# Issue order and PSUM bank of each job from two written tables instead of a list scheduler

## The chip, the cores and the metric

The kernel runs on one core of one Trainium2 chip. The metric is the device time of one execution in microseconds (us); the median of three runs is given.

## The reference

Linear attention of the Linformer kind for 8 batches, 8 heads, 1024 positions and a head width of 64, then a gated feed-forward layer. All inputs and the output are float32.

```python
k_proj = einsum('ks,bhsd->bhkd', E, k)          # 64 projected keys per head
v_proj = einsum('ks,bhsd->bhkd', F, v)
scores = (1/8) * q @ k_proj^T                   # 1024 x 64 per head
attn   = exp(scores - max); attn = attn / (sum(attn) + 1e-9)
x      = attn @ v_proj                          # heads side by side: 8192 x 512
gate   = 1 / (1 + exp(-(x @ w_gate)))           # 512 x 1536
val    = x @ w_val
out    = (gate * val) @ w_out                   # 1536 x 512
```

## The kernel before

Tokens are worked in 16 blocks of 512, two to a batch. Each batch has an attention part: `kv` projects keys and values on TensorE, ScalarE copies the result out (`kd`, `vd`), a transposing DMA or TensorE turns it (`turnk`), `sc` makes the scores of 128 tokens and four heads, VectorE takes the maximum (`top`) and it is subtracted (`sub`, on TensorE or VectorE), ScalarE takes the exponential (`exp`), a DMA turns it (`turnp`), `xo` multiplies by the values, VectorE inverts the sums (`inv`), VectorE or GpSimd divides (`div`), and a DMA turns the result (`turnx`) into the input of the feed-forward part.

The feed-forward matrix products of a block use a Strassen-like scheme with seven products in place of eight (`seven`, L1162). In `quad_jobs` a step has one such scheme for the gate (jobs `G...`) and one for the value (jobs `V...`); the names A11, A12, A22, S1 to S4 tell which product it is. Each product is four matmuls of 256 columns. Between products ScalarE copies a half-made PSUM bank away (`snap`, `copy`), VectorE adds such copies (`plus`), ScalarE takes `tanh`, and VectorE multiplies gate and value (`hidden`). The output product is in `o_jobs` (seven products, jobs `O...` of six matmuls each) or, for the first and last block, in `o_plain` (`Oplain`, twelve matmuls). Results leave PSUM by `leave` and `merge` and go out by `store`.

Work is cut into 2,902 jobs, numbered from 0 in the order in which the code makes them; "sc16" below is job 16, of the kind `sc`. A job has an engine, a position and a body that issues its instructions: 1,054 jobs for TensorE, 712 for ScalarE, 814 for VectorE, 167 for GpSimd (POOL) and 155 for SyncE. Every engine carries out its own jobs strictly in the order in which they are issued. `Plan` (L55) derives every semaphore wait from what each instruction reads and writes, DMAs included, so it needs no change when the order changes.

A job's PSUM result lies in one of 8 banks and its float32 scratch in one of 13 buffers; until the order is known they are `Slot`s, gathered into groups. `Scheduler.run` (L331) sets the order: a list scheduler that keeps a clock for every engine by estimated costs, places the ready job with the lowest position on a free engine, and picks a free bank or buffer (`take`, L264) with a check that no group can lock the others out (`safe`). The positions come from the tables `AT` and `FB` of numbers. Before 25 us of its clock, when TensorE has no ready job, it places a filler: two 128-column matmuls of the identity into bank 7 that nothing reads (`busy(2)`). 45 fillers are placed.

The first batch has a path of its own (`first_batch`, L786): `pk` and `pv` project keys and values as their loads land, `tq` and `tk` turn queries and keys on TensorE, `psum` and `norm` sum and divide on VectorE or GpSimd, `tp` turns the result, `xo0` multiplies by the values; `pkk`, `tqk`, `tkk`, `pvk`, `tpk`, `xok` are the copies out of PSUM. The first block's gate and value products are plain (`plainG`, `plainV`; here G and V with the job's number). `wsum`, `osum`, `xs` and `sum` make the sums that the seven-product scheme needs. Loads of the next batch (`loadkv`, `loadq`) are jobs of GpSimd's queue and wait until the batch before has been turned (`turnx`).

Of the kernel before, what the change touches and what calls it, by code (L numbers as in the profile page):

```python
# [153 lines left out]
class Job:  # L154
    def __init__(self, eng, pos, body, release, name):
        self.eng, self.pos, self.body, self.release, self.name = eng, round(pos, 6), body, release, name
        self.cost, self.bytes, self.dma, self.port = 0.0, 0, False, False
        self.deps, self.slots, self.start, self.end = {}, [], None, None


class Scheduler:

    TAIL = {"PE": 0.0, "ACT": 0.115, "DVE": 0.09, "POOL": 0.15, "SP": 0.0}
    HOP = {"PE": 0.205, "ACT": 0.035, "DVE": 0.035, "POOL": 0.06, "SP": 0.1}

    EXTRA = dict(
        qt=0.12, qt1=0.16, turnk=0.1, turnk0=0.1, tp=0.1, tx=0.1, tk=0.1, tq=0.1, bc0=0.8, den0=0.2, xo0=0.2,
        copyG=0.028, copyV=0.028, copyO=0.028, tanh=0.015, kd=0.1, vd=0.1,
    )

    def __init__(self, banks, bufs, t0, window, landed, busy0, warm):
        self.jobs, self.now, self.t0, self.window, self.landed = [], None, t0, window, landed
        self.busy0, self.warm, self.fillers = busy0, warm, []
        self.writers, self.readers = {}, {}
        self.free = {
            "bank": {b: t0 for b in banks},
            "buf": {b: t0 for b in bufs},
        }
        self.clean = {b: False for b in banks}
        self.groups = []  # L180
        self.reads = []
        self.more = {"ACT": AT["pact"], "DVE": AT["pdve"], "POOL": AT["ppool"]}

    def job(self, eng, pos, body, release=0.0, name=""):
        j = Job(eng, pos, body, release, name)
        self.jobs.append(j)
        self.now = j
        body()
        j.cost += self.EXTRA.get(name, 0.0)
        self.now = None  # L190
        return j

    def note(self, eng, r, w, x, dma, cost, nbytes, port):
        j = self.now
        j.port = j.port or port
        assert eng == j.eng, (eng, j.eng, j.name)
        j.cost += cost
        j.bytes += nbytes
        j.dma = j.dma or dma is not None

        def dep(o, raw):
            if o is not j:
                j.deps[o] = j.deps.get(o, False) or raw

        for k in tuple(r) + tuple(w) + tuple(x):
            if isinstance(k, tuple) and isinstance(k[1], Slot) and k[1] not in j.slots:
                j.slots.append(k[1])
                k[1].left += 1
        for k in r:
            if k in self.writers:  # L210
                dep(self.writers[k], True)
        for k in tuple(w) + tuple(x):
            if k in self.writers:
                dep(self.writers[k], False)
            for o in self.readers.get(k, ()):
                dep(o, False)
        for k in r:
            self.readers.setdefault(k, []).append(j)
        for k in tuple(w) + tuple(x):
            self.writers[k] = j  # L220
            self.readers[k] = []

    def seen(self, o, eng, raw):
        if o.dma:
            return o.end + 0.1
        if o.eng == eng:
            if eng == "PE":
                return o.start + o.cost
            return o.end + 0.02
        if o.eng in ("ACT", "DVE", "POOL") and eng == "PE":  # L230
            return o.end + 0.055
        return o.end + self.HOP[o.eng]

    def safe(self, group, got):
        left = {k: len(f) for k, f in self.free.items()}
        left["clean"] = sum(self.clean[b] for b in self.free["bank"])
        for g, b in got:
            left[g.kind] -= 1
            if g.kind == "bank":
                left["clean"] -= self.clean[b]  # L240
        taken = [g for g, _ in got]
        todo = []
        for g in self.groups + ([] if any(group is x for x in self.groups) else [group]):
            need, held = dict.fromkeys(left, 0), dict.fromkeys(left, 0)
            for x in g:
                if x.at is None and not any(x is y for y in taken):
                    need[x.kind] += 1
                    need["clean"] += x.clean
                elif x.left:
                    held[x.kind] += 1  # L250
                    held["clean"] += x.kind == "bank" and not x.dirty
            todo.append((need, held))
        while todo:
            for i, (need, held) in enumerate(todo):
                if all(need[k] <= left[k] for k in left):
                    for k in left:
                        left[k] += held[k]
                    del todo[i]
                    break
            else:  # L260
                return False
        return True

    def take(self, j, t):  # L264
        got = []
        for s in j.slots:
            if s.at is not None:
                continue
            taken = [b for g, b in got if g.kind == s.kind]
            mine = [b for b, a in self.free[s.kind].items() if a <= t and b not in taken]  # L270
            if s.kind == "bank":
                if s.clean:
                    mine = [b for b in mine if self.clean[b]]
                elif s.dirty:
                    rough = sum(not c for c in self.clean.values()) + sum(self.clean[b] for _, b in got)
                    mine = [b for b in mine if not self.clean[b] or rough < (7 if t < 25.0 else 3)]
                mine.sort(key=lambda b: (self.clean[b], self.free["bank"][b]))
            else:
                mine.sort(key=lambda b: self.free["buf"][b])
            if not mine:  # L280
                return False
            got.append((s, mine[0]))
        if not got:
            return True
        group = got[0][0].group
        if not self.safe(group, got):
            return False
        if not any(group is g for g in self.groups):
            self.groups.append(group)
        for s, b in got:  # L290
            s.at = b
            del self.free[s.kind][b]
            if s.dirty:
                self.clean[b] = False
        return True

    def running(self, j):
        return any(x.group is g for x in j.slots for g in self.groups)

    def place(self, j, t):  # L300
        j.start = t
        j.cost *= 1 + self.more.get(j.eng, 0.0)
        if j.port:
            if j.eng == "DVE":
                j.cost += max(0.0, self.held - t)
                self.lock = t + j.cost
            if j.eng == "POOL":
                j.cost += max(0.0, self.lock - t)
                self.held = t + j.cost
        j.end = t + j.cost + self.TAIL[j.eng]  # L310
        if j.dma:
            begin = max(self.pipe, t + j.cost + 1.3)
            self.pipe = begin + j.bytes / 390e3
            j.end = self.pipe + 0.9 + AT["pdma"]
        self.busy[j.eng] = t + j.cost
        for s in j.slots:
            s.left -= 1
            s.end = max(s.end, j.end + (0.25 if j.eng == "PE" else 0.055))
            if s.left == 0:
                self.free[s.kind][s.at] = s.end  # L320
                if s.kind == "bank" and not s.clean:
                    self.clean[s.at] = not s.dirty
                if all(x.at is not None and not x.left for x in s.group):
                    self.groups = [g for g in self.groups if g is not s.group]
        for k in self.after.get(j, ()):
            self.count[k] -= 1
            if self.count[k] == 0:
                ready = max([self.seen(o, k.eng, raw) for o, raw in k.deps.items()] + [k.release, self.t0])
                self.open[k.eng].append((k.pos, self.rank[k], ready, k))

    def run(self):  # L331
        engines = ("PE", "ACT", "DVE", "POOL", "SP")
        self.busy = dict(self.busy0)
# [4 lines left out]
        for j in self.jobs:  # L338
            self.count[j] = len(j.deps)
            for o in j.deps:  # L340
                self.after.setdefault(o, []).append(j)
# [44 lines left out]
def bass_linformer_attn__then__ffn_glu_sigmoid_kernel(  # L386
# [20 lines left out]
    with contextlib.ExitStack() as es:  # L407
# [62 lines left out]
        NB = 11  # L470
# [1444 lines left out]
```

## Time and profile before

| what | value |
|---|---|
| median of 3 runs | 518.52 us (518.36 to 518.65) |
| span of the profiled execution | 517.0 us |
| median less this span | 1.5 us |
| first matmul to last matmul's end, in the profile | 5.5 to 514.4 us |
| TensorE busy | 508.4 us, 98% |
| VectorE busy | 444.8 us, 86% |
| ScalarE busy | 375.4 us, 73% |
| GpSimd busy | 171.6 us, 33% |
| filler matmuls | 90 of 128 columns |

The profile's times are in microseconds from the start of the span. A row of a timeline gives the start, the time to the end of the last merged instruction, the engine, the source line, the operation, what is written and read, and how many instructions were merged; in brackets, the engine's idle time before it and what ended that. A row of the table of stretches gives the stretch and its length, then the busy time and number of instructions of TensorE, of its weight loads (PEld), of VectorE, ScalarE and GpSimd, then the granted TensorE clock (1.00 is full), the DMA's share in tenths as a mean, and GB/s. L528 is the line of the helper that issues every matmul, L542 of every ScalarE instruction. The profile shows the time to a matmul's modelled end, so consecutive matmuls overlap, and their spacing is read from the starts. The profiled execution has no time of its own beside the span; it is set against the median of the runs.

### The profile page before, as it was taken

Reading aid. Unit: us, or ns where it says so; the run is one execution under the profiler, and the core shown is the slowest. Engines: PE = TensorE matmul, PEld = TensorE weight load, DVE = VectorE, ACT = ScalarE, POOL = GpSimd, SP = SyncE. Lnnn points to the kernel's source line nnn. Section 1 sums busy time; section 2 is a strip of 40 time slices with the busy share of each in tenths; the row PEclk is TensorE's granted clock in tenths of the full one; section 3 lists DMA queues with packets and bytes.
Section 4 is the critical chain, followed back from the end, with each engine's and each line's share of the span. In section 5 each row is a group of like instructions: output and inputs, shape, how many; then the busy total and the mean of one; then the engine's idle time right before and its main releaser. Section 6 shows DMA issues by size and latency. Waiting matters only on the chain.

```text
span 517.0 us, 12313 instructions
## 1 busy us (share of the span) xinstructions
PE 508.4 (98%) x4786; PEld 428.2 (83%) x4786; DVE 444.8 (86%) x843; ACT 375.4 (73%) x715; POOL 171.6 (33%) x200
## 2 busy tenths in 40 slices
PE   5999999999999999999999999999999999999997
PEld 4655867889988898888988889888998889888885
DVE  5879998898999799996999969997999969999570
ACT  1566966879977697777967689776877779677752
POOL 9882004802353024430344313630244303403200
DMA  9999928796689636994489926997369963610204
GB/s 160 198 198 207 202 64 161 117 215 136 123 174 203 161 58 129 187 185 132 82 160 170 191 76 95 188 204 146 77 113 183 202 143 62 145 42 1 82 1 164
DMA packets 140522, 71.59 MB, mean 138 GB/s; under 512 B 97200, under 2 KB 132272, under 8 KB 140464
## 3 DMA queue, kind: packets, MB, share of 16 engines
q0 software_dynamic: 35904, 29.89, 37.4%
q1 hardware_dynamic: 104560, 40.91, 36.9%
q8 instruction: 38, 0.62, 0.5%
q14 instruction: 20, 0.16, 0.1%
HBM read 60.29 MB, written 16.78 MB: 149 GB/s over the span
## 4 chain that ended last, share of the span: by engine, by line
PE 93%; DVE 5%; DMA 1%; ACT 0%; issue 0%; POOL 0%; SPq 0%
PE pA L528 47%; PE pF L528 46%; DVE topf L1645 1%; DVE hT L1066 1%; DMA EF<-in_F_dram 1%; DVE pA L1672 1%; DVE pF L1672 1%; DVE inv L989 0%; ACT KVs L542 0%; POOL wT L996 0%; DVE tG L557 0%; ACT ost L542 0%; DVE inv L990 0%; DVE eT L886 0%; DVE xT L886 0%
## 5 line engine op out<-in xcount | busy, mean ns | idle before, releaser
L542 ACT ACTIVATE spare<-pF 128x512 f32<-128x512 f32 (+2 forms) x167 | 93.7, 572 | 30.5 <-PE pF L528 27.6
L557 POOL TENSOR_TENSOR hT<-hT,hS 128x512 bf16<-128x512 bf16 x42 | 48.6, 1184 | 193.7 <-PE pA L528 155.1
L542 ACT ACTIVATE spare<-pA 128x512 f32<-128x512 f32 (+2 forms) x150 | 85.1, 582 | 15.6 <-PE pA L528 12.0
L542 ACT ACTIVATE spare<-spare 128x512 f32<-128x512 f32 x77 | 48.5, 635 | 25.7 <-DVE spare L1156 25.4
L1734 POOL TENSOR_TENSOR KVs<-spare,inv 128x384 bf16<-128x384 f32 (+1 forms) x50 | 36.6, 738 | 86.9 <-ACT spare L542 43.6
L528 PE MATMUL pA<-wO,hT 128*128 128x256 bf16 (+1 forms) x408 | 60.7, 288 | 0.0
L1225 DVE SCALAR_TENSOR_TENSOR hT<-spare,pF 128x512 bf16<-128x512 f32 x73 | 48.9, 679 | 7.6 <-ACT spare L542 3.6
L528 PEld LDWEIGHTS pA<-wO,hT 128*128 128x128 bf16 x408 | 39.9, 98 | 10.4
L1156 DVE TENSOR_TENSOR spare<-pF,spare 128x512 f32<-128x512 f32 x62 | 41.8, 681 | 3.7 <-PE pF L528 2.0
L528 PE MATMUL pF<-xT,wV 128*128 128x256 bf16 (+1 forms) x276 | 44.7, 283 | 0.0
L528 PE MATMUL pF<-xS,tV 128*128 128x256 bf16 x248 | 37.3, 273 | 0.0
L1156 DVE TENSOR_TENSOR spare<-pA,spare 128x512 f32<-128x512 f32 x53 | 35.7, 676 | 1.3 <-ACT spare L542 0.8
L528 PE MATMUL pA<-xT,wG 128*128 128x256 bf16 (+1 forms) x212 | 34.1, 283 | 0.0
L528 PE MATMUL pF<-xS,wV 128*128 128x256 bf16 x224 | 33.6, 272 | 0.2 <-ACT KVs L542 0.2
L1225 DVE SCALAR_TENSOR_TENSOR hT<-spare,pA 128x512 bf16<-128x512 f32 x41 | 27.7, 679 | 5.8 <-PE pA L528 3.8
L528 PE MATMUL pF<-xT,wG 128*128 128x256 bf16 (+1 forms) x196 | 32.4, 288 | 0.2 <-DVE xT L886 0.2
L528 PEld LDWEIGHTS pF<-xT,wV 128*128 128x128 bf16 x276 | 26.6, 98 | 5.9 <-issue 0.2
L528 PE MATMUL pA<-wT,hT 128*128 128x256 bf16 x240 | 31.1, 272 | 0.0
L1672 DVE TENSOR_TENSOR pF<-pF,topf 128x512 f32<-128x512 f32 x45 | 29.7, 689 | 0.0
L1645 DVE TENSOR_REDUCE topf<-pF 128x8 f32<-128x512 f32 x45 | 29.3, 678 | 0.0
L528 PE MATMUL pF<-wO,hT 128*128 128x256 bf16 (+1 forms) x204 | 29.3, 285 | 0.0
L528 PE MATMUL pA<-wT,hS 128*128 128x256 bf16 x216 | 29.1, 273 | 0.0
(183 smaller groups left out, 1267.0 us busy)
## 6 DMA issues: line engine op xcount, KB each, us to landing
out_dram<-ost SPq DMA_DIRECT2D x63, 256.0 KB, 2.3
KVs<-in_v_dram POOLq DMA_DIRECT2D x15, 512.0 KB, 11.2
KVs<-in_k_dram POOLq DMA_DIRECT2D x14, 512.0 KB, 7.6
Qb<-in_q_dram POOLq DMA_DIRECT2D x14, 512.0 KB, 15.7
wO<-in_moe_w_out_dram POOLq DMA_DIRECT2D x1, 1536.0 KB, 28.5
wG<-in_moe_w_gate_dram POOLq DMA_DIRECT2D x5, 256.0 KB, 16.8
wV<-in_moe_w_val_dram POOLq DMA_DIRECT2D x5, 256.0 KB, 17.5
KVs<-in_k_dram POOLq DMA_DIRECT2D x4, 256.0 KB, 6.8
```

Source lines behind the costliest of these rows:

```text
L528: lambda e: e.matmul(o, lhsT, rhs, **kw),
L542: lambda e: e.activation(o, i, func, scale=scale),
L557: fn = lambda e: e.tensor_tensor(o, a, b, op)
L1066: lambda e: e.scalar_tensor_tensor(hT[0][:, m, :], BF(sg), 1.0, PB(bv)[:, :], ALU.add, ALU.mult),
L1156: lambda e: e.tensor_tensor(PB(b)[:, :] if stay else BF(s), PB(b)[:, :], BF(s), ALU.add),
L1225: lambda e: e.scalar_tensor_tensor(o, y.rearrange("p (j c) -> p j c", j=2), 1.0, x.rearrange("p (j c) -> p j c", j=2), ALU.add, ALU.mult,),
L1645: lambda e: e.tensor_reduce((top if by_pe(b, t, y) else topf)[:, n : n + 8], PB(bk)[:, :].rearrange("p (n k) -> p n k", n=8), mybir.AxisLi ...
L1672: lambda e: e.tensor_tensor(x, x, topf[:, n : n + 8].unsqueeze(2).to_broadcast([P, 8, 64]), ALU.subtract),
L1734: fn = lambda e: e.tensor_tensor(xto.rearrange("p (g h d) -> p h g d", g=2, h=H)[:, hh[0] : hh[1], :, :], o[:, :, 0:DH].rearrange("p (h g) ...
```

## The change

The list scheduler goes. `ORDER`, a table of 2,936 numbers, gives the order in which all jobs are issued (a job's number, or -1 for a filler), and `PLACES`, a table of 906 numbers, gives the bank or buffer of every slot in the order in which the groups are first touched. What each job does, its instructions and their operands' shapes, and `Plan`'s way to derive waits, are as before; waits differ where order, banks or buffers differ. The engine that each job runs on stays. Positions and costs are still handed over, and not read.

```diff
@@ class Job
-    def __init__(self, eng, pos, body, release, name):
-        self.eng, self.pos, self.body, self.release, self.name = eng, round(pos, 6), body, release, name
-        self.cost, self.bytes, self.dma, self.port = 0.0, 0, False, False
-        self.deps, self.slots, self.start, self.end = {}, [], None, None
+    def __init__(self, eng, body, name):
+        self.eng, self.body, self.name, self.slots = eng, body, name, []
+
+ORDER = (
+    0, -1, -1, -1, -1, -1, 1, 2, 3, -1, -1, -1, -1, -1, -1, 14, 4, 15, 12, 5, -1, 6, 13, 16, 22, 17, -1, -1, 7,
+    23, 18, 8, 19, -1, -1, -1, 24, 32, 9, 20, 34, 25, 10, 33, 35, 11, 21, 26, -1, -1, -1, -1, -1, -1, -1, -1,
+    -1, 36, 42, 52, 37, 53, 43, 38, 27, 39, -1, -1, 44, 28, 54, 40, 30, 45, 59, 55, 29, 31, -1, 60, 46, 56, 169,
...
+)
+PLACES = (
+    0, 2, 4, 2, 3, 1, 5, 0, 6, 1, 1, 2, 0, 1, 3, 2, 4, 3, 2, 1, 0, 0, 1, 5, 5, 2, 3, 2, 5, 9, 3, 11, 0, 2, 2, 6,
...
+)
@@ class Scheduler
     def job(self, eng, pos, body, release=0.0, name=""):
...
+        self.jobs.append(Job(eng, body, name))
...
-    def run(self):
...
+    def run(self, fill):
+        groups = []
         for j in self.jobs:
...
+            self.now = j
+            j.body()
+            for s in j.slots:
+                if not any(s.group is g for g in groups[-40:]):
+                    groups.append(s.group)
+        self.now = None
+        slots = [s for g in groups for s in g]
...
+        for s, p in zip(slots, PLACES):
+            s.at = p
+        return [fill if i < 0 else self.jobs[i].body for i in ORDER]
@@ kernel body
-        for j in sched.run():
-            j.body()
+        for body in sched.run(lambda: busy(2)):
+            body()
```

TensorE's order at the start, by job (F x n: n fillers), up to the first output of the plain products:

```
before: pk0 Fx6 pk1 Fx6 tq12 tq14 tk4 Fx3 pk6 F sc16 sc22 Fx2 pk7 sub18 Fx4 sub24 tq32 tq34 tk10 Fx10
        sc36 sc42 pv52 pv53 sub38 tp28 sub44 F pv59 tp30 Fx3 pv60 xo56 Fx3 tp48 Fx5 tp50
        G118 V119 xo63 G112 V113 F G120 V121 G114 V115 G128 V129 G124 tq66 tq68 V125 tq86
after:  pk0 Fx5 pk1 Fx6 tq14 tk4 tq12 F pk6 sc16 sc22 Fx2 pk7 sub18 Fx3 sub24 tq32 tq34 tk10 Fx9
        sc36 sc42 pv52 pv53 sub38 Fx2 sub44 tp28 tp30 pv59 F pv60 xo56 Fx3 tp48 Fx2 tp50
        V119 G112 xo63 V113 G118 G128 G124 G120 V129 G114 V121 V125 tq68 tq66 V115 tq86
```

VectorE's and ScalarE's in the same stretch:

```
VectorE before: ... psum20 tqk35 psum26 norm21 top37 top43 norm27 tpk29 psum40 psum46 norm41 pvk61 norm47 pvk62 tpk51
VectorE after:  ... psum20 tqk35 norm21 psum26 top37 top43 norm27 psum40 tpk29 psum46 norm41 norm47 pvk61 pvk62 tpk51
ScalarE before: exp19 pkk9 exp25 tqk33 tkk11 pvk54 exp39 exp45 pvk55 tpk31 xok57 xok58 tpk49 xok64
ScalarE after:  exp19 pkk9 exp25 tqk33 tkk11 exp39 pvk54 exp45 pvk55 tpk31 xok58 xok57 tpk49 xok64
```

Over the whole kernel, jobs that stand at another place in their engine's own order: TensorE 858 of 1,054 (3.4 places on average over all, at most 30), ScalarE 531 of 712 (2.2), VectorE 640 of 814 (3.0), GpSimd 115 of 167 (1.4), SyncE 87 of 155 (1.1). There are 34 fillers, all ahead of job tp50.

More of the change, by code (lines that the diff above doesn't have):

```diff
@@ L154, with __init__, note @@
 class Job:
-    def __init__(self, eng, pos, body, release, name):
-        self.eng, self.pos, self.body, self.release, self.name = eng, round(pos, 6), body, release, name
-        self.cost, self.bytes, self.dma, self.port = 0.0, 0, False, False
-        self.deps, self.slots, self.start, self.end = {}, [], None, None
-class Scheduler:
[L163 to L182, printed above, removed]
-    def job(self, eng, pos, body, release=0.0, name=""):
[L185 to L193, printed above, removed]
-        j = self.now
[L195 to L203, printed above, removed]
+    def __init__(self, eng, body, name):
+        self.eng, self.body, self.name, self.slots = eng, body, name, []
+ORDER = (
[154 rows of a table added]
+)
+PLACES = (
[26 rows of a table added]
+)
+class Scheduler:
+    def __init__(self):
+        self.jobs, self.now = [], None
+    def job(self, eng, pos, body, release=0.0, name=""):
+        self.jobs.append(Job(eng, body, name))
+    def note(self, eng, r, w, x):
+        j = self.now
+        assert eng == j.eng
         for k in tuple(r) + tuple(w) + tuple(x):
@@ L207, in note @@
                 j.slots.append(k[1])
[L208 to L329, printed above, removed]
```

64 lines of the change are left out of this document (3 added, 61 removed), and 176 rows, old and new, of tables (ORDER, PLACES).

## The prediction

> **What bounds the kernel now.** I read the page first (busy times, then the chain), then a table of stretches, then TensorE's timeline where the table shows a hole, and VectorE's at the start.
>
> From the page, busy time by engine:
>
> ```profile
> PE 508.4 (98%) x4786; PEld 428.2 (83%) x4786; DVE 444.8 (86%) x843; ACT 375.4 (73%) x715; POOL 171.6 (33%) x200
> ```
>
> From the table of stretches (TensorE is the first figure after the length):
>
> ```profile
> 0.00:25.00 25.00, 19.43 (x240) 14.49 (x240) 17.70 (x48) 8.97 (x16) 22.56 (x38) 1.00 1.24 178
> 25.00:50.00 25.00, 24.77 (x186) 13.46 (x183) 21.05 (x44) 15.21 (x28) 15.16 (x15) 1.00 1.35 202
> 112.50:173.40 60.90, 60.90 (x588) 53.59 (x586) 57.05 (x105) 47.81 (x93) 19.73 (x22) 1.00 0.88 164
> 234.10:294.80 60.70, 60.70 (x586) 53.41 (x585) 54.63 (x103) 47.01 (x91) 19.74 (x22) 1.00 0.78 146
> ```
>
> A busy PE can hide small waits, so I take the spacing of starts instead. The chain has this row:
>
> ```profile
> 58.11 1.31 PE pF L528 x12
> ```
>
> Twelve 256-column matmuls in 1.31 us are 109 ns each. One steady period holds 504 of them (6 steps of 14 products of 4, two output blocks of 14 jobs of 6), 55.0 us; 16 of the k/v projection, 1.9; 32 score and 32 output jobs, 3.7 together: 60.6 us against the 60.7 of a period. So the steady part has some 0.1 us a period to give. Adding the spacing of every matmul from the first gate product at 23.73 us on, and comparing with where it really starts, the lag grows to 2.5 us over the run: 0.19 at a filler at 25.9, 0.40 at 49.20, 0.32 at 80.34, about 0.05 twice a period (0.6 in all), 0.8 where the array changes between full tiles and halves (which any order pays), the rest in 0.05s. The two large ones, in TensorE's timeline:
>
> ```profile
> 48.37 0.60 PE L528 MATMUL pF<-xT,wV 128*128 128x256 bf16 x4
> 49.20 0.61 PE L528 MATMUL pF<-xT,wG 128*128 128x256 bf16 x4 [0.23 <-DVE xT L886]
> 79.80 0.39 PE L528 MATMUL pA<-kpD,qT 128*128 128x128 bf16 x4
> 80.34 0.60 PE L528 MATMUL pF<-xS,wV 128*128 128x256 bf16 x4 [0.16 <-ACT KVs L542]
> ```
>
> The first 23.7 us are another matter: 45 fillers of two matmuls (`pA<-ident`) hold the place of work that is not ready. The same view there:
>
> ```profile
> 7.36 1.06 PE L528 MATMUL pF<-KVs,EFT 128*64 128x256 bf16 x8
> 8.36 1.46 PE L528 MATMUL pA<-ident 128*128 128x128 bf16 x12
> 9.75 1.06 PE L528 MATMUL pF<-KVs,EFT 128*64 128x256 bf16 x8
> 10.75 0.86 PE L528 MATMUL pA<-ident 128*128 128x128 bf16 x12
> 13.11 0.28 PE L528 MATMUL pA<-ident 128*128 128x128 bf16 x2
> 13.23 0.61 PE L528 MATMUL pA<-kpD,qT 128*128 128x128 bf16 x8
> 16.34 1.28 PE L528 MATMUL pA<-ident 128*128 128x128 bf16 x20
> 23.50 0.40 PE L528 MATMUL pF<-ident,wT 128*128 128x128 bf16 x4
> 25.91 0.28 PE L528 MATMUL pA<-ident 128*128 128x128 bf16 x2
> ```
>
> What sets the pace there is VectorE, which from 13.65 to 24.4 goes almost without a break. Its timeline:
>
> ```profile
> 21.09 0.63 DVE L989 TENSOR_REDUCE inv<-spare 128x8 f32<-128x512 f32 x1
> 21.87 0.64 DVE L996 TENSOR_TENSOR wT<-spare,inv 128x512 bf16<-128x512 f32 x1
> 22.43 0.41 DVE L886 CAST vpD<-pF 64x256 bf16<-64x256 f32 x1
> 22.77 0.67 DVE L996 TENSOR_TENSOR wT<-spare,inv 128x512 bf16<-128x512 f32 x1
> ```
>
> The last row ends at 23.44, and the transposition that reads it (tp50) starts at 23.50.
>
> **The change, part by part.** The instructions other than fillers are the same; only order and place differ. The sum is made against the profiled execution, a span of 517.0 us; the median 518.5 has 1.5 us around it, which I leave.
>
> *Start.* 45 fillers become 34. At 58 ns a matmul (12 in 10.75 to 11.45) the 11 are worth 1.2 us if all were in the way, nothing if what follows waits for data anyhow; these are the ends. Walking the new order with the old durations: one filler fewer before pk1, at the cold spacing of 116 ns, gives 0.23 (8.36 + 10 x 0.116 = 9.52 against 9.75). tk4 moves between tq14 and tq12, and the filler between pk6 and sc16 is gone, so sc16 waits for tqk13 alone, about 12.95 against 13.23. These 0.28 us go down VectorE's and ScalarE's queues to sub38 (18.90 against 19.18). Then pvk54 on ScalarE comes behind exp39, which holds exp45 back (20.23 against 20.10), and tpk29 gets between the two row sums on VectorE, +0.1; norm47 passes ahead of pvk61, -0.34. tp50 comes at about 23.3: -0.2. tp28, tp30, pv59 and pv60 also leave TensorE earlier, which covers pvk61's delay, as xo063 now has a second product in front. I take -0.3, nearer to the walk than to the 1.2.
>
> *The filler at 25.91.* V113 is now followed by products that were later, so the filler goes (-0.18); but G128, the third of them, takes a bank that xok65 empties at 1.26 us after xo063's start, 0.1 short. Net -0.1 (ends 0 and -0.2).
>
> *The wait at 49.20.* G262 took bank 3, which xok111 (VectorE, ended 49.15) had just emptied. In the new table its bank is 5, last used over 2 us before. -0.4; nothing takes its place within two jobs.
>
> *The wait at 80.34.* The S1 product 284 takes the bank of sc337, whose exponential (exp340) ended at 80.20, behind its maximum and subtraction on VectorE. By matmul time sc337 to product 284 is 3.9 us in the old order and 4.6 in the new (Oplain423 and product 275 come between), so the 0.32 fits into the 0.66 gained. -0.3 (ends 0, if VectorE comes to exp340's operands as much later, and -0.3).
>
> *A new wait.* tq86 takes the bank of tq68, two matmul jobs and one product earlier; ScalarE's copy of tq68 (0.6 us, ended 0.67 after tq68's last matmul in the old trace) makes it 0.16 to 0.3 late: +0.2.
>
> *Steady periods.* Seven to eight in ten jobs of every engine but SyncE stand at another place in their queue, by 1 to 3 places on average. I compared, from the tables, how much matmul time lies between the product that feeds a PSUM read and the job that needs its bank or result, less the read's own row: under 0.2 us in 26 places before, 28 after; under 0.5 us in 188 and 160. So handovers are not thinner. The two 0.05s a period (OA12 behind mergeO, VA22 behind snapV) go mostly, 0.6; some ten similar ones come (GA22 behind snapG, VS3 behind snapV): +0.4. Other 0.05s: -0.1. Net -0.3, bounded by -0.8, where all go, and by the second rival below.
>
> *DMA queues.* POOL's and SyncE's queues are reordered too. Loads of one batch trade places inside their batch; the K and V loads that kv301 and kv294 need land by 44.5 and 62.0 us before, the same bytes go first now, and kv294 keeps over a microsecond. At no cost, with one exception (third rival). The last four output tiles and their stores stand in the same order, so the 2.6 us after the last matmul stay.
>
> Sum: -0.3 - 0.1 - 0.4 - 0.3 + 0.2 - 0.3 = -1.2 us: span 515.8, median **517.3**.
>
> **Rivals.**
> 1. *The start gives nothing and small waits come back.* For it: the first products hang on K, Q and V landings, and the walk gained 0.2 only; ten new thin handovers. Against: 49.20 and 80.34 are plain bank clashes and gone. +0.2 at tq86, -0.4 in the middle: about 518.3.
> 2. *Slower: VectorE's queue becomes what TensorE waits for.* In the first period VectorE is busy 57.05 of 60.90 us, in the others 54.6 of 60.7, and 640 of its 814 jobs stand elsewhere. A product that closes a bank (VS4) moves up to 11 us later, so its bank is held that much longer; a job at the head of VectorE's queue that waits for it stops all behind. One such stop a period of half a `plus` row (0.68 us) would be 0.34 x 7.5 = 2.6 us, and a little more on the last blocks: 520.0. It decides from 0.16 a period, where the gain is used up; 0.3 makes it slower by over 0.2%. Against: 6 us of slack a period, and the handovers counted above, though that count sees no queue.
> 3. *A projection that waits for its loads.* kv659 stands 7.2 us of matmuls earlier in TensorE's order, at 166.4 instead of 173.63, or 165.5 with the gains. Its last load was issued at 150.84 and landed 12.8 later, 163.6, and the output job that frees the buffer (xo644) is 1.3 us later, so 164.9: 0.6 us remain. Loads 2 us later still would cost 1.4: 518.7.
>
> ```profile
> 148.57 1.56 POOL L569 DMA_DIRECT2D KVs<-in_k_dram  x2 [0.89 <-DMA xT<-KVs]
> 150.11 1.51 POOL L569 DMA_DIRECT2D KVs<-in_v_dram  x2
> ```
>
> 4. *The array slows down without its fillers.* Matmuls of 128 columns start 116 ns apart at 8.36 and 58 ns apart from 10.75 on. If the quieter start brought the slow spacing back once for as long as it lasted at first (5.49 to 10.75), that is half of 5.3: 519.9. Against it: the longest hole that the new table can leave is under half a microsecond. [...]
>
> **How the numbers follow.** Forecast 0.50 (its own range 516.5 to 518.0); rival 1 0.17; rival 2 0.26; rival 3 0.05; rival 4 0.02. 0.2% (1.0 us) is about what a measurement of this kernel can tell. Three quarters of the forecast lie below 517.5, with a little of rival 1: faster 0.40. The rest of the forecast, rivals 1 and 3: same 0.31. Rivals 2 and 4 with the tail of 3: slower 0.29. Range 516.4 (start and steady part both near their better ends) to 520.0 (half of rival 2), leaving out 0.05 and 0.14.
>
> **What would show it.** Right: sc16 near 12.95 and tp50 near 23.3; no hole before the gate product at 49 us or the S1 product at 80; a hole of 0.2 before tq86; periods of 60.7 or less. Wrong: periods of 61 or more with TensorE waiting for VectorE reads; kv659 with a hole ahead; a start as late as before.

## The result and the profile after

| | before | after |
|---|---|---|
| median, same chip and session | 518.59 us (518.36 to 519.34) | 521.13 us (520.58 to 522.83) |
| span of the profiled execution | 517.0 us | 518.8 us |
| first transposition of the last start step (tp50) | 23.50 us | 22.67 us |
| last matmul's end to the end of the span | 2.64 us | 2.65 us |

The changed kernel is slower: the ratio is 1.0053, 95% interval 1.0036 to 1.0069, some 2.5 us. The forecast was 517.3 us, and the range ended at 520.0. The profiled execution shows 1.8 us of it: its tp50 came 0.83 us earlier than before, and most of that lead is luck of the one execution (the twelve matmuls, below).

The busy times on the page of the kernel after:

```profile
PE 507.4 (98%) x4760; PEld 426.1 (82%) x4764; DVE 446.1 (86%) x843; ACT 375.0 (72%) x715; POOL 169.9 (33%) x200
```

Its table of stretches, whose columns are those of the table shown of before:

```profile
173.40:234.10 60.70, 59.70 (x576) 52.22 (x574) 55.82 (x103) 44.90 (x87) 19.29 (x22) 1.00 0.76 146
234.10:294.80 60.70, 60.70 (x586) 54.10 (x586) 54.00 (x104) 46.29 (x89) 19.79 (x22) 1.00 0.74 143
294.80:355.50 60.70, 59.79 (x578) 52.78 (x575) 54.53 (x99) 48.35 (x94) 19.53 (x22) 1.00 0.72 136
```

The first and the last of these three stretches in the kernel before:

```profile
173.40:234.10 60.70, 60.70 (x586) 53.41 (x585) 54.63 (x103) 47.01 (x91) 19.73 (x22) 1.00 0.76 142
294.80:355.50 60.70, 60.70 (x586) 53.41 (x585) 54.62 (x103) 47.06 (x91) 19.73 (x22) 1.00 0.78 145
```

TensorE still works 98% of the span, and the granted clock reads 1.00. But two of the periods, which had been full to 60.70 of 60.70 before, now hold 59.70 and 59.79: about a microsecond each. The view of TensorE's waits names what they were for (columns: engine, what waits, what it waited for, us in total, times, longest):

```profile
PE pF L516 <- DVE hS L545: 1.0, 1, 1.0
PE pA L516 <- DVE hS L545: 0.9, 1, 0.9
```

Both are waits for `hS`, the operand that VectorE's `sum` jobs make for the output product OS2; before, the view of waits had no such line. (This view counts from the modelled end of the matmul before; the table below counts from the start that the spacing would have allowed, and so has 1.17 and 1.07.) Here is TensorE's timeline of the first one, in the kernel after:

```profile
212.44 0.60 PE L516 MATMUL pA<-xS,tV 128*128 128x256 bf16 x4
214.04 0.83 PE L516 MATMUL pF<-wT,hS 128*128 128x256 bf16 x6 [1.00 <-DVE hS L545]
```

VectorE's timeline of the same stretch, kernel after:

```profile
211.52 2.47 DVE L545 TENSOR_TENSOR hS<-hS,hT 128x1024 bf16<-128x1024 bf16 x1
```

And GpSimd's, kernel after:

```profile
210.70 1.55 POOL L557 DMA_DIRECT2D KVs<-in_v_dram  x2 [4.18 <-DMA xT<-KVs]
212.25 1.17 POOL L545 TENSOR_TENSOR xS<-xT,xS 128x512 bf16<-128x512 bf16 x1
```

The same work in the kernel before, on VectorE (two sums in one row), GpSimd and TensorE:

```profile
211.98 1.02 DVE L557 TENSOR_TENSOR hS<-hS,hT 128x1024 bf16<-128x1024 bf16 x2
207.00 1.39 POOL L557 TENSOR_TENSOR xS<-xT,xS 128x512 bf16<-128x512 bf16 x1 [2.19 <-DVE xS L557]
213.66 0.82 PE L528 MATMUL pA<-wT,hS 128*128 128x256 bf16 x6
```

In the kernel after, one add (sum21269: job 1269, of the kind `sum2`) took 2.47 us; the same form takes 0.68 or 0.69 elsewhere. It ended at 213.99, 0.56 after GpSimd's add (xs1036) had ended at 213.43. At 334.5 us something alike happened: sum22006 and sum22005 took 1.26 (0.42 elsewhere) and 1.64 us around xs1772, and the second ended at 336.46, 0.56 after GpSimd's 335.90. In the old table xs1036 stood ahead of its batch's loads in GpSimd's queue and was over at 208.4; the new table has it behind two loads, which wait for turnx1016, and so it ran beside the sums.

By the sum of spacings that the prediction used, TensorE's lag from tp50 to the end is 5.16 us against 2.53 before. The holes that make it up are in this table (profiled execution; the second column is the kernel before).

| place | before | after |
|---|---|---|
| filler, then product 120 or 128, at 25 us | 0.19 | 0.19 |
| tq86, 31.28 us | 0 | 0.29 |
| gate or value product on the bank of xok111, 49 us | 0.40 | 0.34 |
| S1 product 284, 80 us | 0.32 | 0 |
| product 499, 91.6 us, behind a turn's landing | 0 | 0.20 |
| scores sc565, sc569, 123 to 126 us | 0 | 0.18 |
| OS2, 214.04 and 336.51 us | 0 | 1.17 + 1.07 |
| sc2409, 428.8 us | 0 | 0.14 |
| all else | 1.62 | 1.58 |

TensorE's timeline of the kernel after at the two places that the prediction showed of before:

```profile
48.36 0.60 PE L516 MATMUL pA<-xT,wG 128*128 128x256 bf16 x4
49.14 0.61 PE L516 MATMUL pF<-xT,wV 128*128 128x256 bf16 x4 [0.18 <-DVE xT L867]
...
79.48 0.61 PE L516 MATMUL pF<-xS,wG 128*128 128x256 bf16 x4
79.92 0.60 PE L516 MATMUL pA<-xS,wV 128*128 128x256 bf16 x4
```

The gate product 262 (48.36) now runs without a wait, and the value product 278 right behind it waits for the bank that xok111 empties, as 262 did before. Product 284 (79.92) follows its neighbour at the spacing of 0.44 us: that wait is gone.

### The profile page after: what moved, and what is told of

It reads as the page before. It is cut to its first block, busy times and chain, and to the rows that moved or that the text cites. A ratio compares the mean times of both kernels' runs of the same rounds, so it can differ in the third digit from the quotient of the medians.

```text
span 518.8 us, 12197 instructions
## 1 busy us (share of the span) xinstructions
PE 507.4 (98%) x4760; PEld 426.1 (82%) x4764; DVE 446.1 (86%) x843; ACT 375.0 (72%) x715; POOL 169.9 (33%) x200
## 4 chain that ended last, share of the span: by engine, by line
PE 95%; DVE 2%; ACT 1%; DMA 1%; issue 0%; SPq 0%
PE pF L516 52%; PE pA L516 43%; DVE hS L545 1%; DMA EF<-in_F_dram 1%; ACT EF L530 0%; DVE hT L1047 0%; ACT spare L530 0%; DVE ost L1395 0%; DVE hT L545 0%; ACT vpD L530 0%; DVE xT L867 0%; DVE pF L1137 0%; DVE pA L1137 0%; ACT eT L530 0%; DVE hT L1206 0%
## 5 line engine op out<-in xcount | busy, mean ns | idle before, releaser
L1715 POOL TENSOR_TENSOR KVs<-spare,inv 128x256 bf16<-128x256 f32 (+1 forms) x48 | 34.5, 727 | 94.1 <-PE pA L516 37.2
L516 PE MATMUL pF<-wO,hT 128*128 128x256 bf16 (+1 forms) x358 | 53.4, 290 | 0.1
L516 PEld LDWEIGHTS pF<-wO,hT 128*128 128x128 bf16 x360 | 34.9, 98 | 9.5
L516 PE MATMUL pA<-wO,hT 128*128 128x256 bf16 (+1 forms) x250 | 35.3, 282 | 0.1
L516 PE MATMUL pA<-xT,wV 128*128 128x256 bf16 (+1 forms) x216 | 35.0, 284 | 0.0
L516 PE MATMUL pA<-xS,tG 128*128 128x256 bf16 x224 | 33.6, 273 | 0.0
L516 PE MATMUL pF<-wT,hT 128*128 128x256 bf16 x240 | 31.7, 272 | 0.0
L516 PE MATMUL pA<-xS,wV 128*128 128x256 bf16 x200 | 30.0, 273 | 0.0
L516 PEld LDWEIGHTS pA<-wO,hT 128*128 128x128 bf16 x252 | 24.5, 98 | 5.4
L516 PE MATMUL pF<-wT,hS 128*128 128x256 bf16 x204 | 27.2, 273 | 1.0 <-DVE hS L545 1.0
```

Source lines behind the costliest of these rows:

```text
L516: lambda e: e.matmul(o, lhsT, rhs, **kw),
L1715: fn = lambda e: e.tensor_tensor(xto.rearrange("p (g h d) -> p h g d", g=2, h=H)[:, hh[0] : hh[1], :, :], o[:, :, 0:DH].rearrange("p (h g) ...
```

## The experiments

Theory C, formed on this trace: an add of VectorE whose two operands lie in SBUF is held up by such an add of GpSimd at the same time; the new order puts two of these clashes on sums that TensorE is about to need. Rival Q: VectorE's queue is fuller where these sums stand, and GpSimd's add has little to do with it. Theory D, for the smaller loss at 123 us: the turns (transposing DMAs) stand behind stores in SyncE's queue.

**The changed kernel once more.**

> The changed kernel once more. Its four executions spread from 520.6 to 522.8 us, those of before from 518.4 to 519.3. Theory C: the holes at the two sums are in this profile too, and what differs between executions is which VectorE adds meet a GpSimd add, so that other holes of 0.5 to 1.5 us show where such a meeting falls. Theory Q: the same small holes everywhere, a little longer each.

Measured in a second session, beside the next three, 521.12 us against 518.87 (ratio 1.0034, 1.0020 to 1.0047). The two OS2 holes were there again, 1.13 and 1.07; the one at sc565 and sc569 was 0.47 and 0.30 in place of 0 and 0.18, so this second loss varies between executions.

**GpSimd's two adds ahead of their loads.**

```diff
 GpSimd's queue (same places)
-loadkv1020 loadkv1019 xs1036 loadkv1017
+xs1036 loadkv1020 loadkv1019 loadkv1017
-loadkv1755 loadkv1754 loadkv1753 xs1772 loadq1758
+xs1772 loadkv1755 loadkv1754 loadkv1753 loadq1758
```

> The changed kernel with two GpSimd jobs, xs1036 and xs1772, put back ahead of their batch's loads, as before the change; all else as changed. Theory C (collision): in the changed kernel the adds sum21269 and sum22005/22006 on VectorE ran 2.47, 1.64 and 1.26 us in place of 0.69, 0.69 and 0.42 because GpSimd's add ran beside them, and TensorE waited 1.17 and 1.07 us for them. Then both holes go: 2.2 us less than the changed kernel, about 518.9 us, not slower than before by more than 0.2%. Theory Q (VectorE's queue order as such makes TensorE wait): the holes are only refilled elsewhere, the time stays above 520.5 us.

Measured: 519.33 us (ratio 1.0007, 0.9998 to 1.0016). Both holes at OS2 are gone. VectorE's timeline of this kernel at the same place:

```profile
213.10 0.68 DVE L542 TENSOR_TENSOR hS<-hS,hT 128x1024 bf16<-128x1024 bf16 x1
```

GpSimd's, this kernel:

```profile
208.66 1.16 POOL L542 TENSOR_TENSOR xS<-xT,xS 128x512 bf16<-128x512 bf16 x1 [0.97 <-DVE xS L542]
211.91 1.55 POOL L554 DMA_DIRECT2D KVs<-in_v_dram  x2 [2.08 <-issue]
213.44 1.50 POOL L554 DMA_DIRECT2D KVs<-in_k_dram  x2
```

The same add takes 0.68 us now, though GpSimd issues loads all through it: loads alone do not hold it up. What is left over the kernel before lies mostly at sc565 (0.74) and sc569 (0.39).

**Only the start of the new table, and only the rest of it.** Two halves: the new order and places up to tp50 with the old ones behind it, and the reverse.

> The new order and places up to job tp50 (the first 23 us, 34 fillers), the old order and places from there on. In the changed kernel tp50 began at 22.67 us against 23.50. Theory C: the start is a gain by itself and the loss lies in the steady part: 0.83 us less than before, about 517.8 us, less some 0.1 where the weights land later than the earlier product wants them. Theory S (start): the earlier start brings loads and products into a worse rhythm and part of the loss comes from it: 518.5 us or more.

Measured: 518.45 us (ratio 0.9989, 0.9979 to 0.9999). This is less than the 0.8 us that C expected: the 0.83 at tp50 came from one execution of each kernel (in this one tp50 stands at 23.60, against 23.50 before).

> The old order up to tp50 (44 of the 45 fillers), the new order and places from there on. Theory C: the two holes of 1.1 us stay and the start's 0.8 us are lost: 521.5 to 522 us. Theory S: without the new start the rest does no harm, 519 us or less.

Measured: 521.44 us (ratio 1.0045, 1.0032 to 1.0059), with holes of 0.84 and 1.07 at OS2, and a wait of 0.4 us for a V load at a projection at 420.57 in this execution. The start is worth about -0.4 us (-1.1 to -0.1 by the interval), the rest costs about 2.6.

**The clash put into the kernel before.** Nothing of the new table, only GpSimd's add two loads later in five periods:

```diff
 GpSimd's queue, also at xs668, xs1404, xs1772, xs2140
-xs1036 loadkv1017 loadkv1018 loadkv1019
+loadkv1017 loadkv1018 xs1036 loadkv1019
```

> The kernel before with one thing changed: in five periods the GpSimd add of the MoE input (xs668, 1036, 1404, 1772, 2140) stands behind two K and V loads in GpSimd's queue in place of ahead of them, so that it runs beside VectorE's sums, as two of them do in the changed kernel. Theory C (an add of VectorE with both operands in SBUF waits while such an add of GpSimd runs, and the sums feed the OS2 product, which has 1.0 us of margin in each of these periods): the four sums of a period end 1.2 to 1.8 us later, so 0.2 to 0.8 us per period come out as holes ahead of OS2, together 1.0 to 4.0: 519.9 to 522.9. Theory Q (the sums in the changed kernel are late because VectorE's queue is fuller there, and GpSimd's add matters little): no hole over 0.1 us at OS2, 518.4 to 519.2.

Measured: 524.38 us (ratio 1.0103, 1.0089 to 1.0117), more than the 522.9 that C allowed. VectorE's timeline of this kernel:

```profile
211.28 2.69 DVE L543 TENSOR_TENSOR hS<-hT 128x1024 bf16<-128x1024 bf16 x2
213.90 1.01 DVE L543 TENSOR_TENSOR hS<-hS,hT 128x1024 bf16<-128x1024 bf16 x2
```

GpSimd's, this kernel:

```profile
211.89 1.19 POOL L543 TENSOR_TENSOR xS<-xT,xS 128x512 bf16<-128x512 bf16 x1
```

TensorE's, this kernel:

```profile
214.63 0.83 PE L514 MATMUL pA<-wT,hS 128*128 128x256 bf16 x6 [0.57 <-DVE hS L543]
```

Two sums take 2.69 us in place of 1.02, and OS2 loses 0.62 to 0.84 in three of the five periods, and in a fourth 0.43 ahead of its fifth matmul, as expected. What C had not counted is the rest of VectorE's queue: the jobs behind the sums run late too, and the products at 216.8, 218.3 and 218.9 us lose 0.17, 0.16 and 0.16 more, again in every later period.

**VectorE's order mended, GpSimd's left alone.**

```diff
 VectorE's queue of the changed kernel
-sum21270 sum31271 plusV1099 sum21269
+sum21269 sum21270 sum31271 plusV1099
-plusV1835 sum12004 sum22006 sum22005
+sum12004 sum22005 sum22006 plusV1835
```

> The changed kernel with GpSimd's queue left alone, and VectorE's order mended at the two places: sum21269 two jobs earlier, sum22005 and sum22006 ahead of plusV1835, so that they are over before GpSimd's adds begin at 212.25 and 334.51 us. Theory C: both holes ahead of OS2 (1.1 us each) go, GpSimd's adds fall on other adds that nobody waits for, and the time is that of the version with GpSimd's adds moved, 519.3 (519.0 to 519.9). If instead the earlier GpSimd adds helped that version by what they did to the loads and not by the collision (theory Q), the time stays at 521 or over.

Measured: 520.10 us (ratio 1.0017, 1.0007 to 1.0027), one microsecond better than the changed kernel, 0.2 worse than the range expected. Both holes at OS2 are gone. But GpSimd's add now hits the next sum in VectorE's queue, and somebody waits behind this one too. VectorE's timeline of this kernel:

```profile
212.14 2.62 DVE L542 TENSOR_TENSOR hT<-hT 128x1024 bf16<-128x1024 bf16 x1
214.69 0.68 DVE L1134 TENSOR_TENSOR pA<-pA,spare 128x512 f32<-128x512 f32 x1
```

GpSimd's, this kernel:

```profile
213.03 1.17 POOL L542 TENSOR_TENSOR xS<-xT,xS 128x512 bf16<-128x512 bf16 x1
```

TensorE's, this kernel:

```profile
216.96 0.61 PE L513 MATMUL pF<-xS,tV 128*128 128x256 bf16 x4 [1.29 <-ACT pA L527]
```

The `sum3` ends at 214.76, again 0.56 after GpSimd's 214.20. Three jobs behind it hidden1190 empties a bank late, ScalarE's copy into that bank (copyV1252) starts at 216.33 and the product at 216.96 is 1.45 us late. At 334 us GpSimd's add still stretched a sum that TensorE waits for (sum22006, 1.38 us from 334.89 on, 0.42 elsewhere), but OS2 followed at 336.81 without a hole. So the delay follows GpSimd's add from one sum to the next, which is what C says and Q does not; that nobody would wait for the add it meets instead was C's error.

**The second batch's turns ahead of the stores**, on top of GpSimd's mended queue:

```diff
 SyncE's queue
-turnq406 store563 store562 turnq405 turnk412 turnq408 turnq407 store561
+turnq406 turnq405 turnk412 turnq407 turnq408 store563 store562 store561
```

> The version with the two GpSimd adds ahead of their loads, and in SyncE's queue around the second batch the turns of Q and K ahead of the three stores that the new table put among them (turnq407 also ahead of turnq408). Theory D (the score products at 123 and 125.7 us wait for turns that stand behind two stores of 0.94 and 0.42 us and behind another turn of 1.3 us): turnk412 lands some 1.4 us and turnq407 some 2.7 us earlier, both holes (0.74 and 0.39 us there) go, the time falls by 0.6 to 1.1 us against that version's 519.3: 518.2 to 518.7. Theory L (the turns are late because their loads landed late, and the queue's order is not what counts): the holes stay within 0.3 us of their size, 519.2 to 519.6.

Measured: 518.46 us (ratio 0.9993, 0.9984 to 1.0002). No hole is left at 123 to 126 us. SyncE's queue in the changed kernel (second session):

```profile
116.54 1.59 SPq L1293 DMA_DIRECT2D out_dram<-ost  x2
118.17 1.30 SPq L1474 DMA_TRANSPOSE qT<-Qb  x1
119.57 1.47 SPq L1517 DMA_TRANSPOSE kpD<-kpd  x1
121.14 2.66 SPq L1474 DMA_TRANSPOSE qT<-Qb  x2
```

SyncE's queue in this kernel:

```profile
114.16 3.31 SPq L1471 DMA_TRANSPOSE qT<-Qb  x2
117.57 1.28 SPq L1514 DMA_TRANSPOSE kpD<-kpd  x1
118.94 2.67 SPq L1471 DMA_TRANSPOSE qT<-Qb  x2
121.67 1.55 SPq L1290 DMA_DIRECT2D out_dram<-ost  x3
```

The two stores held the queue for 1.59 us ahead of the turns that the scores need; without them the key's turn (`kpD`) ends by these rows at 118.85 in place of 121.04 (some 0.7 of that is the earlier start of this execution, tp50 at 22.59 against 23.31). D holds. With the two mendings the changed table is level with the kernel before.

**The old order with the new start and the two bank waits taken out.** Product 262 takes bank 5 in place of 3; product 284 goes ahead of sc341, in bank 7 in place of 2; from there on the two banks of each pair change roles.

> The old order and places with three parts of the new idea: the start of the new table up to the first transposition of the gate's weights; the gate product 262 in the bank that has been free for 1.7 us (banks 3 and 5 change roles from there on); the S1 product 284 ahead of score product 341, in the bank free since 79.7 us (banks 2 and 7 change roles). Theory of bank clashes (both waits are the bank alone): the holes of 0.40 at 49.2 and 0.32 at 80.3 us go and nothing takes their place, so with the 0.4 of the start 518.45 falls by 0.7 to 517.7 (517.4 to 518.0). Rival (the waits move to the next job, as the one at 49.2 did in the changed kernel): 518.3 to 518.7.

Measured: 518.18 us (ratio 0.9988, 0.9979 to 0.9997), between the two theories. The hole at 49 us went for good. At 80 us product 284 started at 80.13, still 0.27 late: the bank was free at 79.77, but its weights' sum (wsum195) ended on VectorE at 80.07. The 0.32 had a second wait in its shadow, and moving the product ahead of sc341 made it larger: in its old place, at 80.02, the same sum, which ended at 80.01 in the kernel before, would have cost some 0.05.

**The changed table with both mendings and two more banks.** tq86 and product 278 get banks that had been free for longer. (This kernel and the next do not compute the reference: a part of their result is wrong. By the tables, copyV215 and copyV279 lie there, and in no other kernel here, in a bank last used by transpositions and by products on parts of the array; that this is the cause was not tried. The instructions are the same in kind and number.)

> The new table with GpSimd's two adds ahead of their loads and the second batch's turns ahead of the stores (518.46 in the run before), and two more places changed: tq86 in the bank that gate0123 left at 30.14 us (banks 0 and 2 change roles from there on), the gate product 278 in the bank that gate0135 left at 48.40 (banks 2 and 6 change roles). Theory of bank clashes: the holes of 0.29 at 31.2 and 0.34 at 49.1 go, 0.6 us in all: 517.8 (517.5 to 518.1), under the kernel before's 518.8. Rival (what stood in their shadow comes up, as wsum195 did when product 284 was moved): 518.2 to 518.6.

Measured: 518.14 us (ratio 0.9985, 0.9977 to 0.9994): the holes of 0.29 and 0.34 went, and 0.39 at product 499 (0.13 in the run before) and 0.26 at 50 to 51 us came up in this execution. Half way between the theory and its rival; the 0.3 gained over the run before is within the intervals of the two.

**Twelve matmuls ahead of the first work.** tp50 lay between 22.59 and 23.67 us in the profiles so far, with the old start as with the new one. What goes with it is the moment at which the spacing of 128-column matmuls drops from 107 to 56 ns. TensorE's timeline in the kernel after:

```profile
8.59 1.00 PE L516 MATMUL pA<-ident 128*128 128x128 bf16 x10
9.52 0.63 PE L516 MATMUL pF<-KVs,EFT 128*64 128x256 bf16 x8
10.07 0.84 PE L516 MATMUL pA<-ident 128*128 128x128 bf16 x12
12.39 0.62 PE L516 MATMUL pA<-kpD,qT 128*128 128x128 bf16 x8
```

TensorE's timeline in the kernel with only the new start, whose order of work is the same here:

```profile
8.45 1.25 PE L514 MATMUL pA<-ident 128*128 128x128 bf16 x10
9.63 1.06 PE L514 MATMUL pF<-KVs,EFT 128*64 128x256 bf16 x8
10.63 1.30 PE L514 MATMUL pA<-ident 128*128 128x128 bf16 x12
13.33 0.62 PE L514 MATMUL pA<-kpD,qT 128*128 128x128 bf16 x8
```

The eight projection matmuls take 0.63 or 1.06, the twelve fillers 0.84 or 1.30, and sc16 stands at 12.39 or 13.33.

```diff
+        busy(12)
         project_consts()
```

> The same kernel with 12 matmuls of the identity (128 columns, nobody reads them) ahead of TensorE's first work, from 4.0 us on, when the identity is there, to 5.4, when the first data lands. Theory W (the start of every execution depends on the moment at which the spacing of 128-column matmuls drops from 107 to 56 ns, which lay at 9.2, 10.8 or 11.6 us in the profiles so far, 3.4 to 6.0 us after the first matmul): the moment comes up to 1.4 us earlier, to 7.4 to 10.2 us, and tp50, 22.6 to 23.6 so far, to 22.0 to 23.0: 0.4 to 0.7 us less than without, about 517.3, with less spread. Rival D (the start goes by when the loads land; the spacing follows the work): no change over 0.15 us.

Measured: 518.42 us (ratio 0.9990, 0.9981 to 0.9998), no better than without them (518.14), and not the 517.3 of theory W. The moment did come earlier, to 8.37 us, and sc16 to 11.95, the earliest of all; but tp50 stood at 23.02, because a value projection (pv52) then waited for its load, which landed at 17.66, and all behind it with it. W is right on the spacing and wrong on what the time does here.

> The kernel before with the same 12 matmuls ahead, nothing else. Theory W: tp50 at 22.3 to 23.3 in place of 23.0 to 23.7, the time 0.3 to 0.7 us less, 518.1 to 518.5, with less spread. Rival D: 518.7 to 519.0.

Measured: 518.42 us (ratio 0.9989, 0.9980 to 0.9997), all executions between 518.03 and 518.72; the drop in the profile came at 9.48 us, tp50 at 23.04. As W expected, though the interval allows from 0.2 to 1.0 us.

**The best of the old order.** The new start, the two banks, wsum195 one job earlier and the twelve matmuls:

> The old order with the new start and the two mended places (518.18 before), the weight sum wsum195 one job earlier in VectorE's queue, so that product 284 waits 0.2 us less for it, and the 12 matmuls ahead of the first data. If the early matmuls take the late cases of the start away, as they did in the kernel before (518.89 to 518.42), 517.7 (517.4 to 518.0), under the kernel before by 0.2% and more. Rival: in the new start the V loads, which land at 17.7 us, hold sub38 and with it tp50 at 23.0 whatever the early matmuls do, as in the new table with them (tp50 at 23.02): then only the late half of the cases gains, 517.9 to 518.2.

Measured: 518.14 us against 519.00 in its session (ratio 0.9981, 0.9972 to 0.9990): faster than both kernels, by 0.2% of the kernel before, and within the rival's range. Not by the rival's cause, though: in the profile product 284 follows almost at once (79.59, its neighbour at 79.11), the load ahead of pv52 had landed at 16.98, a microsecond before its use, and the drop came only at 10.75 us in spite of the early matmuls, with tp50 at 23.29. The early matmuls do not fix the moment, and the run is not told apart from the one without its last two parts (0.9988).

## Why the prediction was wrong

Term by term, as the prediction put them:

- *Start, -0.3.* Right in size at tp50. At the same moment of the drop the new start is 0.3 us ahead (tp50 at 22.67 against 22.97, drops at 9.25) or 0.2 (23.31 against 23.50, drops at 10.8 and 10.9), and alone it gave -0.4. Not by the route described, though: from sc16 to tp50 it is 10.27 or 10.28 us in every profile with either start (11.07 in the one where pv52 waited for its load), so norm47's step ahead of pvk61 gave nothing, and all of it lies before sc16. A tenth is lost again behind tp50: the first product follows 0.34 us later in the new order, 0.23 in the old. The agreement in size is therefore partly luck. (The fillers' 116 ns hold one longer last step: they start 107 ns apart, so the filler less ahead of pk1 is worth 0.21, not 0.23.) And sc16 "near 12.95" said too much: it moves by 1.0 us (12.31 to 13.34) from one execution to the next.
- *Filler at 25.91, -0.1.* Its zero end: 0.19 before and after.
- *Wait at 49.20, -0.4.* Wrong. "Nothing takes its place within two jobs" was said of the bank's user, and looked only at the next bank of product 262. The next product in TensorE's order, 278, took the bank that xok111 empties: 0.34.
- *Wait at 80.34, -0.3.* Right: gone, and by the route described: product 284 again has the bank of sc337, and exp340 ended at 79.46 in place of 80.20. That wsum195, of which the prediction did not speak, also ended earlier (79.75 in place of 80.01), and so ahead of the product, was luck.
- *tq86, +0.2.* Right: 0.29.
- *Steady periods, -0.3.* The step that failed. The count of handovers looked at PSUM reads only; one of the two OS2 of a period gets its operand through SBUF from a sum with 1.0 to 1.1 us to spare before, and so was in no count. And it took each row's duration as fixed, though the order decides what runs beside it. The small waits it did speak of stayed where they were (1.62 and 1.58 us). In their place came 2.2 us at OS2.
- *DMA queues, at no cost.* Wrong by 0.1 to 1.1 us: only loads and the last stores were looked at, not the stores that the new table puts between turns in SyncE's queue; product 499 loses 0.2 to a turn's landing as well.

With the measured values the sum is -0.3 + 0 - 0.1 - 0.3 + 0.3 + 2.2 and 0.4 to 1.3, for the turns and product 499: +2.2 to +3.1. The difference of the medians, 2.5, lies in between; since the turns vary so much between executions, the sum cannot be set against it more closely.

Of the rivals, the second named the right engine and the right sign, but not the mechanism: at neither hole did a job at the head of VectorE's queue wait for a late product, and the loss is no even 0.34 a period but two clashes of about 1.1 us. The third did not happen: kv659 started at 166.12, as forecast, with no wait. The fourth did not happen either: past 12 us no 128-column matmuls start 107 ns apart again, and the usual step is 56 (55 or 56 in 296 of 308 steps). (The granted clock reads 1.00 ahead of the drop too, from 7 to 9 us in both kernels, so it could not have shown this.) What the first said of the middle (-0.4) was as far off as the forecast.

The trace of before did show what was needed. VectorE's timeline of the kernel before, at 165 us, has a clash of the same form, on an `xs` add behind which TensorE shows no hole:

```profile
164.83 1.29 DVE L557 TENSOR_TENSOR xS<-xS,xT 128x512 bf16<-128x512 bf16 x1
166.05 0.68 DVE L1156 TENSOR_TENSOR spare<-pF,spare 128x512 f32<-128x512 f32 x1
```

GpSimd's, kernel before:

```profile
164.69 1.15 POOL L557 TENSOR_TENSOR hT<-hT,hS 128x512 bf16<-128x512 bf16 x1
166.20 1.16 POOL L557 TENSOR_TENSOR xS<-xT,xS 128x512 bf16<-128x512 bf16 x1 [0.36 <-DVE xS L557]
```

An add that takes 0.41 us elsewhere took 1.29, to 0.28 after GpSimd's end; the add with one operand in PSUM ran beside the next GpSimd add at its usual 0.68. The rest of that trace reads the same: of the 17 bf16 adds of VectorE with both operands in SBUF that ran beside an add or a division of GpSimd, 16 took 0.67 to 1.37 us in place of 0.41 or 0.42; the 39 f32 adds of 512 columns with one operand in PSUM that shared at least 0.3 us with one took 0.65 to 0.69, against 0.67 to 0.70 where GpSimd had none. With that row and GpSimd's order beside VectorE's sums, the two clashes might have been found from the tables; that walk was not made.

There was a second clue, in the code that the change removes: the list scheduler marks VectorE's jobs without a PSUM operand and GpSimd's adds as `port`, and `place` (L300) lengthens such a job's estimate by the time for which the other engine's is still running. In the kernel before, none of the sums for `hS` was stretched; the `xs` adds were. The groups by form (count, then busy us and mean ns), kernel before:

```profile
L557 DVE TENSOR_TENSOR xS<-xT 128x512 bf16<-128x512 bf16 x30 | 18.4, 631 | 0.5 <-DMA xT<-KVs 0.5
L557 DVE TENSOR_TENSOR xS<-xS,xT 128x512 bf16<-128x512 bf16 x15 | 12.1, 810 | 0.0
L557 DVE TENSOR_TENSOR hS<-hS,hT 128x1024 bf16<-128x1024 bf16 x14 | 9.6, 683 | 0.0
```

Kernel after:

```profile
L545 DVE TENSOR_TENSOR xS<-xT 128x512 bf16<-128x512 bf16 x30 | 15.2, 519 | 0.9 <-DMA xT<-KVs 0.9
L545 DVE TENSOR_TENSOR xS<-xS,xT 128x512 bf16<-128x512 bf16 x15 | 7.1, 473 | 0.1
L545 DVE TENSOR_TENSOR hS<-hS,hT 128x1024 bf16<-128x1024 bf16 x14 | 12.3, 882 | 0.2
```

Against 0.41 and 0.69 us an add, the `xs` adds were stretched by some 12 us in all before and 4 after, and the sums by nothing before and some 4 after (1.7 of it in 512-column ones, not shown). So VectorE lost less time to these clashes than before, but in rows that TensorE was about to need. Whether the old order owes this to the estimates was not tried.

## What to carry to other kernels

When an order changes, a row's duration is not a constant (one add took 2.47 us here and 0.68 once GpSimd's add had been moved): list which rows were stretched by a neighbour before, and which had to be spared, and ask which rows the new order puts beside that neighbour. Count handovers through SBUF with the same care as those through PSUM, and walk the DMA queues for what stands ahead of a landing that TensorE needs, stores included. A wait that is removed has to be followed past the job that had it: to the next user of the same bank, and to the operand that was late in its shadow.

## What the runs showed of the hardware

- In these cases the stretched adds end 0.56 us after GpSimd's for the 1,024-column add (at 213.99, 336.46, 214.76 and, in the kernel with the clash put in, 213.64), 0.28 for the 512-column one (166.12, kernel before). Those are the adds' own 0.69 and 0.41 us less 0.13, so by the rows nearly the whole add runs after GpSimd's.
- By the recorded starts VectorE's add was the first one in three of these cases, by 0.61 to 0.89 us (211.52 against 212.25), in two of them time enough to be over, and it still ended 0.56 us after GpSimd's. And sum22006, begun at 333.63, ended at 334.90 in the middle of GpSimd's recorded add, which itself took 1.39 us in place of 1.16. What held VectorE ahead of the recorded GpSimd adds was not settled. In each of these cases GpSimd was issuing a load just ahead of its add, but load issues alone held up nothing (19 such adds of VectorE beside them in the kernel after, none stretched: 0.41 or 0.42 us for 512 columns, 0.68 or 0.69 for 1,024).
- The drop of the spacing came 3.4 to 6.1 us after the first matmul, at 9.2 to 11.7 us, in kernels without early matmuls (5.72 and 9.25 in the kernel after, 5.49 and 10.8 in the kernel before); with them, which begin at 4.08, it came at 8.37, 9.48 and 10.75, that is 4.3 to 6.7 us after the first. In the new start tp50 moves by 1.0 us with it (22.59 with the drop at 9.2, 23.60 at 11.7). That it makes most of the spread between executions of one kernel is likely, but not shown, as one execution of each was traced. The granted clock reads 1.00 ahead of the drop as behind it; what makes the spacing drop, and what sets the moment, these rows do not show.
